# Other places for the Sinkhorn steps of the second mixture, and a branch hint for TensorE

## The chip, the cores and the metric

One core of a Trainium2 chip runs the whole program in one launch. The metric is the device time of that launch in microseconds, the median of several runs.

## The reference

Three layers follow each other, all in float32:

```
phi(x) = [exp(p - max|p|), exp(-(p - max|p|))],  p = x @ w_phi
x   = phi attention of q, k, v (2 batches, 8 heads, 576 tokens, 64 wide) -> 1152 tokens x 512
x   = moe(x):   each token goes to the expert of its largest logit, at most `capacity` of them
                per expert (288 here); out = gate * relu(x @ w1[e]) @ w2[e]; dropped tokens are 0
logits = x @ w_gate2;  P = exp(logits - logits.max())
for 8 rounds:  P /= P.sum(1) + 1e-9;  P /= P.sum(0) + 1e-9;  P *= N / E
out = sum over e of P[:, e] * (relu(x @ w1[e]) @ w2[e])      (8 experts, 512 -> 1024 -> 512)
```

The matrix products of the mixtures are done in float32 accuracy by splitting each operand into a high and a low part and adding three products.

## The kernel before

The order of the program is the order of the code: nothing reorders it, and each engine works through its own list.

**First mixture.** The loop over `jobs` handles one expert at a time. A branch on the expert's token count picks `job_wide` or `job_narrow` (the profile's input takes `job_narrow` in the last job). Each job lays its tokens in columns of `x2H` and `x2L`, so that the kept tokens stand together.

**Second mixture.** A last branch on the number of kept tokens, `with tc.If(kept_r > N - P)` (L1133), picks `moe2_all` or, here, `moe2_fast`, which works on the first 1024 columns only. The two bodies lie one behind the other in each engine's program.

`moe2_fast` goes through 32 *units*, four per expert, each a quarter of the expert's hidden columns. `first_plain` is unit 0: four groups of 12 matmuls (`three`, L198 to L200) make the hidden blocks; between them stand the gate's logits (`gate2`, L598 and L600, 24 matmuls), copied out by `sink_logits` (L829), and the two `mix` generators (L972 to L988), which make the sums and differences of the token blocks that the later units multiply. Then come the first four second-layer products of unit 0 (`second`, 6 matmuls each, one token tile of 128 each).

`unit(g)`, for g from 1 to 31, makes its hidden blocks by seven products `prod` (L995, 6 matmuls each) in a scheme with fewer multiplications, in three PSUM banks pA, pB, pC. After each product it calls `side(k)`, k from 0 to 6, and `side(7)` at the end. `side(k)` first issues one `second` of the unit before (only four of them in unit 1, at k from 0 to 3), then weight work (`prep2`, `prep`), then maybe a Sinkhorn step. VectorE and ScalarE turn the products into `hidH` and `hidL` (`relu_split`, L1030 and L1031).

The Sinkhorn work is a list `pending` of twelve steps, taken from the front: `sink_start` (nine transposes L839 on TensorE, then four small VectorE operations to the per-partition maximum), `sink_max` (transpose L848, then L849), `sink_exp` (small product L853, then L854, L855 and ScalarE's L856), `sink_row` (four VectorE operations, L859 to L862), and eight `sink_col` (product L867, L868, L869, then the next `sink_row`, or at the last the gate factor). Each step needs the one before, and the steps with a product make TensorE wait for VectorE. They are taken at t = 2 and 3 of `first_plain` and then at every odd k of `side`: two in unit 0, four in each of units 1 and 2, two in unit 3. The matrix `Pm` that they make is first used in unit 4, where the sums of expert 0 are scaled (`gates`).

Of the kernel before, what the change touches and what calls it, by code (L numbers as in the profile page):

```python
# [20 lines left out]
def kernel(  # L21
# [621 lines left out]
    with ExitStack() as mctx:  # L643
# [19 lines left out]
        def win_T(j, c):  # L663
# [5 lines left out]
                    ps[:, a * WP:(a + 1) * WP], xw[:, a, c * P:(c + 1) * P], ident[0:WP, 0:WP])  # L669
            split2(*x1[c], ps)  # L670

        def job_wide(j, off_r):
            i, w = jobs[j]
            for kk, f in enumerate(FO):
                ps = bank(W)
                for c in range(NC):
                    three(ps, wt.w1(f, c), x1[c], c, NC)
                evict_split(h1H[:, kk, :], h1L[:, kk, :], ps, relu=True)
                if i > 0 and kk < 4 and w == 0:
                    wt.split(i, 1, kk)  # L680
            pg = prep(0)
            for d in range(NC):
                ps = bank(W)
                for kk, f in enumerate(FO):
                    wH, wL = wt.w2(f)
                    three(ps, (wH[:, d * P:(d + 1) * P], wL[:, d * P:(d + 1) * P]),
                          (h1H[:, kk, :], h1L[:, kk, :]), kk, NFC)
                evict_split(x2H[:, d, ds(off_r, W)], x2L[:, d, ds(off_r, W)], ps)
                for c in ((0, 1), (2,), (3,), ())[d]:
                    win_T(j + 1, c)  # L690
                if d == 2:
                    win_load(j + 2)
                if w == NW - 1:
                    if i + 1 < E:
                        wt.split(i + 1, 0, d)
                    else:
                        next(pg)

        def job_narrow(j, off_r):
            i, w = jobs[j]  # L700
            pool = {(1, 3), (0, 1), (0, 3)}

            pg = prep(0)

            def split(i, which, p):
                if i == E:
                    next(pg)
                else:
                    wt.split(i, which, p, nc.gpsimd if (which, p) in pool else None)

            def turn_h(g):
                ps = bank4()
                for f in range(4):
                    o = f % 2 * P
                    nc.tensor.transpose(ps[:, f, :], hn[2 * g + f // 2][:, o:o + P], ident)
                split2(h1H[:, 4 * g:4 * g + 4, 0:P], h1L[:, 4 * g:4 * g + 4, 0:P], ps)

            if i > 0:
                split(i, 1, 0)
            for p in range(4):  # L720
                ps = bank(256)
                for c in range(NC):
                    three(ps, (x1[c][0][:, 0:P], x1[c][1][:, 0:P]), wt.w1p(p, c), c, NC)
                nc.scalar.activation(out=hn[p], in_=ps, func=AF.Relu)
                if i > 0 and p < 3:
                    split(i, 1, p + 1)
                if p == 1:
                    ring["n"] += 1
                if p == 2:
                    turn_h(0)  # L730
            win_T(j + 1, 0)
            win_T(j + 1, 1)
            turn_h(1)
            ring["n"] += 1
            split(i + 1, 0, 0)
            split(i + 1, 0, 1)
            for g in range(2):
                ps = bank(256)
                for kk, f in enumerate(FO):
                    wH, wL = wt.w2(f)  # L740
                    n = slice(g * 256, (g + 1) * 256)
                    three(ps, (h1H[:, kk, 0:P], h1L[:, kk, 0:P]), (wH[:, n], wL[:, n]), kk, NFC)
                nc.scalar.activation(out=yn[g], in_=ps, func=AF.Copy)
                if g == 0:
                    win_T(j + 1, 2)
                    split(i + 1, 0, 2)
            win_T(j + 1, 3)
            win_load(j + 2)
            ring["n"] += 1
            ps = bank4()  # L750
            for c in range(NC):
                o = c % 2 * P
                nc.tensor.transpose(ps[:, c, :], yn[c // 2][:, o:o + P], ident)
            split(i + 1, 0, 3)
            split2(x2H[:, :, ds(off_r, P)], x2L[:, :, ds(off_r, P)], ps)
# [180 lines left out]
    def moe2_fast(fp):  # L936
# [64 lines left out]
        def second(g, t):  # L1001
            e, p = divmod(g, 4)
            ps = pb[3 + nout[0] % 4]
            nout[0] += 1
            w = [sp1[2 * (g % 2) + x].rearrange("p (a n) -> p a n", a=2) for x in range(2)]
            n = slice(t % 4 * P, (t % 4 + 1) * P)
            for k in range(2):
                hH, hL = made[g][f"{k + 1}{t // 4 + 1}"]
                three(ps, (hH[:, n], hL[:, n]), (w[0][:, k, :], w[1][:, k, :]), k, 2)
            while gates and gates[0][0] <= nout[0]:  # L1010
                _, o, gate = gates.pop(0)
                nc.scalar.activation(out=o, in_=o, func=AF.Copy, scale=gate)
            o = oc[t]
            gate = Pm[:, t, e:e + 1]
            if g == 0:
                nc.scalar.copy(o, ps)
            elif e == 0:
                nc.vector.tensor_tensor(out=o, in0=ps, in1=o, op=ALU.add)
                if p == 3:
                    gates.append((nout[0] + 4, o, gate))  # L1020
            else:
                nc.vector.scalar_tensor_tensor(out=o, in0=ps, scalar=gate, in1=o, op0=ALU.mult, op1=ALU.add)  # L1022
            if g == 4 * E - 1:
                put(t)

        pending = [sink_start, sink_max, sink_exp, sink_row] + [lambda it=it: sink_col(it) for it in range(8)]

        def relu_split(dst, src):
            hi, lo = dst
# [4 lines left out]
        def first_plain():  # L1034
# [25 lines left out]
            for t in range(4):  # L1060
                second(0, t)
                if t < 2:
                    next(ms[1])
                else:
                    pending.pop(0)()
            return [slots[4], slots[5]]

        def unit(g, spare, todo):
# [10 lines left out]
            def side(k):  # L1079
                if todo:  # L1080
                    second(g - 1, todo.pop(0))
                if k == 0:
                    prep2(g)
                    if g + 1 < 4 * E:
                        pg[0] = prep(g + 1, stmp)
                if pg[0] and 1 <= k <= 4:
                    next(pg[0])
                    if k == 4:
                        wt.load(E + (g + 1) // 4 + 1, 0, (g + 1) % 4)
                if k % 2 and pending:  # L1090
                    pending.pop(0)()
                if g == 3 and k == 5:
                    for t in range(8, NT):
                        nc.gpsimd.memset(oc[t], 0.0)
                        put(t)
# [34 lines left out]
    def put(t):  # L1130
        scatter("out", out, tokc[:, t, 0:1], oc[t])

    with tc.If(kept_r > N - P) as cmp:  # L1133
        with tc.tile_pool(name="h2p", bufs=1) as h2p:
            moe2_all(h2p)
    with cmp.Else():
# [30 lines left out]
```

## Time and profile before

| what | value |
|---|---|
| median of 3 runs | 1029.74 us (1029.55 to 1030.85) |
| the profiled execution's own time | 1028.67 us |
| its span in the trace | 1027.0 us |
| mean granted clock of TensorE | 0.974 |
| busy: PE, DVE, ACT, POOL | 966.4, 604.6, 372.3, 412.9 us |

The stages in the profile's time: attention up to about 140 us, the first mixture from 147 to 337 us, the branch at 337 to 341 us, unit 0 to about 371 us, unit 1 to 394 us, unit 2 to 418 us, then about 20.4 us a unit to the end. PE is TensorE's matmuls, PEld its weight loads, DVE is VectorE, ACT ScalarE, POOL GpSimd. A time in brackets at a row's end is the idle time of the engine ahead of that row, with what ended it; "issue" means that nothing the profile shows was waited for.

### The profile page before, as it was taken

To read this page: it belongs to the slowest core of one execution; us is meant where nothing else is said; L and a number is where in the kernel's file an instruction comes from. 1 tells how busy PE (TensorE), PEld (TensorE's weight loads), DVE (VectorE), ACT (ScalarE), POOL (GpSimd) and SP (SyncE) were. 2 spreads that over 40 slices of the span, in tenths; PEclk is the share of its full clock that TensorE was granted. 3 is DMA by queue.
4 is the path that set the end of the run, shared out by engine and by line. 5 is a ranking of instruction groups with operands and counts; after the bars stand their busy time and mean duration, and the time that the engine had idled before them with its cause. 6 is when DMAs were issued, how large, how long until landed. Compare 5 with 4: busy or idle time off the path is not lost.

```text
span 1027.0 us, 14033 instructions
## 1 busy us (share of the span) xinstructions
PE 966.4 (94%) x5329; PEld 841.8 (82%) x5329; DVE 604.6 (59%) x1074; ACT 372.3 (36%) x621; POOL 412.9 (40%) x398
## 2 busy tenths in 40 slices
PE   8999969978888878999999999999999999999997
PEld 8999968968877656888888888888888888888886
DVE  4667764656554557855565556555655565556555
ACT  4456513566365332233223222322232223222320
POOL 2344243023033535435533553455345434543433
PEclk9999989999998889999999999999999999999999
DMA  7697121579686201111211221122112211110002
GB/s 125 150 276 236 62 89 31 179 212 241 200 230 192 79 21 62 51 41 56 68 42 41 61 63 42 41 62 62 41 41 62 63 41 42 61 41 1 1 1 82
DMA packets 123292, 89.68 MB, mean 87 GB/s; under 512 B 34528, under 2 KB 101344, under 8 KB 123200
## 3 DMA queue, kind: packets, MB, share of 16 engines
q1 hardware_dynamic: 120240, 83.65, 28.9%
q0 software_dynamic: 1728, 4.73, 1.2%
q8 instruction: 55, 0.90, 0.4%
q14 instruction: 37, 0.30, 0.1%
q10 hardware_dynamic: 1232, 0.10, 0.1%
HBM read 79.01 MB, written 9.45 MB: 86 GB/s over the span
## 4 chain that ended last, share of the span: by engine, by line
PE 80%; issue 8%; DVE 7%; ACT 2%; POOL 2%; DMA 1%; ACTq 0%; POOLq 0%; DVEq 0%; SPq 0%
PE pb L995 27%; PE pb L198 15%; PE pb L199 14%; PE pb L200 14%; PE pb L310 3%; PE pb L445 3%; PE pb L428 1%; POOL out_dram L177 1%; DVE hidL L1031 1%; PE pb L254 1%; PE pb L668 1%; DMA wg<-in_moe_w_gate_dram 0%; DVE w1L L158 0%; DVE x2L L801 0%; DVE dq L291 0%
## 5 line engine op out<-in xcount | busy, mean ns | idle before, releaser
L1022 DVE SCALAR_TENSOR_TENSOR oc<-pb,Pm,oc 128x512 f32<-128x512 f32 x224 | 167.1, 749 | 93.8 <-PE pb L200 91.5
L949 POOL TENSOR_TENSOR w1L<-raw,w1H 128x1024 fp32r<-128x1024 f32 x32 | 77.2, 2412 | 345.7 <-ACT w1H L948 345.7
L198 PE MATMUL pb<-w1H,hidH 128*128 128x512 f32 x512 | 199.8, 390 | 0.5 <-DVE hidL L1031 0.5
L199 PE MATMUL pb<-w1L,hidH 128*128 128x512 f32 x512 | 199.7, 390 | 0.0
L200 PE MATMUL pb<-w1H,hidL 128*128 128x512 f32 x512 | 199.6, 390 | 0.0
L1030 ACT ACTIVATE hidH<-snap 128x512 fp32r<-128x512 f32 x93 | 58.8, 632 | 240.7 <-DVE snap L1110 110.1
L995 PE MATMUL pb<-x2H,w0H 128*128 128x512 f32 x310 | 122.6, 396 | 0.0
L995 PE MATMUL pb<-x2L,w0H 128*128 128x512 f32 x310 | 121.7, 392 | 0.0
L995 PE MATMUL pb<-x2H,w0L 128*128 128x512 f32 x310 | 121.5, 392 | 0.0
L198 PEld LDWEIGHTS pb<-w1H,hidH 128*128 128x128 f32 x512 | 96.5, 189 | 20.7 <-DVE hidL L1031 0.6
L199 PEld LDWEIGHTS pb<-w1L,hidH 128*128 128x128 f32 x512 | 96.4, 188 | 20.1
L200 PEld LDWEIGHTS pb<-w1H,hidL 128*128 128x128 f32 x512 | 96.4, 188 | 20.1
L1031 DVE SCALAR_TENSOR_TENSOR hidL<-snap,hidH 128x512 fp32r<-128x512 f32 x93 | 65.7, 706 | 65.0 <-ACT hidH L1030 65.0
L640 POOL TENSOR_TENSOR w0L<-stmp,w0H 128x1024 fp32r<-128x1024 f32 x31 | 74.8, 2414 | 1.6 <-DMA raw<-in_moe_w_dram 1.6
L995 PEld LDWEIGHTS pb<-x2H,w0L 128*128 128x128 f32 x310 | 58.8, 190 | 12.4
L995 PEld LDWEIGHTS pb<-x2H,w0H 128*128 128x128 f32 x310 | 58.7, 189 | 11.9
L995 PEld LDWEIGHTS pb<-x2L,w0H 128*128 128x128 f32 x310 | 58.8, 190 | 11.8
L158 POOL TENSOR_TENSOR w1L<-raw,w1H 128x1024 fp32r<-128x1024 f32 x9 | 21.5, 2384 | 109.5 <-ACT w1H L155 109.2
L635 POOL TENSOR_TENSOR w0L<-raw,w0H 128x512 fp32r<-128x512 f32 x64 | 64.7, 1033 | 0.2 <-ACT w0H L624 0.2
L1030 ACT ACTIVATE hidH<-pb 128x512 fp32r<-128x512 f32 x35 | 20.9, 597 | 96.2 <-PE pb L995 91.3
L1098 ACT COPY snap<-pb 128x512 f32<-128x512 f32 x31 | 18.2, 587 | 83.7 <-PE pb L995 83.7
L995 PE MATMUL pb<-w1H,w0L 128*128 128x512 f32 x124 | 48.3, 389 | 0.0
(246 smaller groups left out, 1999.9 us busy)
## 6 DMA issues: line engine op xcount, KB each, us to landing
raw<-in_moe_w_dram SPq DMA_DIRECT2D x128, 256.0 KB, 3.5
raw<-in_moe_w_dram SPq DMA_DIRECT2D x64, 512.0 KB, 3.8
xe<-zero SPq DMA_DIRECT2D x18, 256.0 KB, 4.2
xw<-xe SPq DMA_DIRECT2D x7, 576.0 KB, 6.9
v<-in_v_dram SPq DMA_DIRECT2D x8, 256.0 KB, 4.9
q<-in_q_dram SPq DMA_DIRECT2D x8, 256.0 KB, 5.2
k<-in_k_dram SPq DMA_DIRECT2D x7, 256.0 KB, 4.9
xw<-xe SPq DMA_DIRECT2D x4, 144.0 KB, 2.5
```

The costliest lines, as they stand in the source:

```text
L198: nc.tensor.matmul(ps, lhsT=aH, rhs=bH, start=i == 0, stop=False)
L199: nc.tensor.matmul(ps, lhsT=aH, rhs=bL, start=False, stop=False)
L200: nc.tensor.matmul(ps, lhsT=aL, rhs=bH, start=False, stop=i == n - 1)
L310: nc.tensor.matmul(kvps[b][g // 4][:, g % 4, 0:MW], lhsT=kp[:, h, half, :], rhs=vv[:, h * VW:h * VW + MW], start=first and g % 4 == 0, sto ...
L445: nc.tensor.matmul(ps[:, h, 0:MW], lhsT=qt[:, g, :], rhs=kv[b][:, g * KW:g * KW + MW], start=half == 0, stop=half == 1,)
L635: tt(out=aL[:, o, :], in0=w, in1=aH[:, o, :].bitcast(F32), op=ALU.subtract)
L640: tt(out=sL, in0=wide(tmp), in1=sH.bitcast(F32), op=ALU.subtract)
L949: nc.gpsimd.tensor_tensor(out=lo, in0=r, in1=hi.bitcast(F32), op=ALU.subtract)
L995: nc.tensor.matmul(o, lhsT=a[x][:, c, :], rhs=b[c][y], start=first and c == 0 and m == 0, stop=c == 1 and m == 2, skip_group_check=True)
L1022: nc.vector.scalar_tensor_tensor(out=o, in0=ps, scalar=gate, in1=o, op0=ALU.mult, op1=ALU.add)
L1030: nc.scalar.activation(out=hi, in_=src, func=AF.Relu)
L1031: nc.vector.scalar_tensor_tensor(out=lo, in0=src, scalar=0.0, in1=hi.bitcast(F32), op0=ALU.max, op1=ALU.subtract)
```

## The change

First, the Sinkhorn steps are taken at twelve set places, pairs (unit, k) in a table `sink_at`, and no longer in `first_plain`. Second, the last branch gets a label, and at the head of the last job, in both of its bodies, TensorE is told which way that branch will go (a value computed from `kept_r`). An assertion says that the gate scaling comes after the last step.

```diff
@@ -669,8 +669,13 @@
                     ps[:, a * WP:(a + 1) * WP], xw[:, a, c * P:(c + 1) * P], ident[0:WP, 0:WP])
             split2(*x1[c], ps)
 
+        def hint(j):
+            if NW == 1 and j == len(jobs) - 1:
+                tc.mark_branch_hint_location("moe2", hint=kept_r > N - P, engines=[ENG.PE])
+
         def job_wide(j, off_r):
             i, w = jobs[j]
+            hint(j)
             for kk, f in enumerate(FO):
                 ps = bank(W)
                 for c in range(NC):
@@ -698,6 +703,7 @@
 
         def job_narrow(j, off_r):
             i, w = jobs[j]
+            hint(j)
             pool = {(1, 3), (0, 1), (0, 3)}
 
             pg = prep(0)
@@ -1009,6 +1015,7 @@
                 three(ps, (hH[:, n], hL[:, n]), (w[0][:, k, :], w[1][:, k, :]), k, 2)
             while gates and gates[0][0] <= nout[0]:
                 _, o, gate = gates.pop(0)
+                assert not pending
                 nc.scalar.activation(out=o, in_=o, func=AF.Copy, scale=gate)
             o = oc[t]
             gate = Pm[:, t, e:e + 1]
@@ -1024,6 +1031,7 @@
                 put(t)
 
         pending = [sink_start, sink_max, sink_exp, sink_row] + [lambda it=it: sink_col(it) for it in range(8)]
+        sink_at = ((1, 3), (1, 6), (2, 0), (2, 1), (2, 3), (2, 5), (2, 7), (3, 1), (3, 3), (3, 5), (3, 7), (4, 1))
 
         def relu_split(dst, src):
             hi, lo = dst
@@ -1061,8 +1069,6 @@
                 second(0, t)
                 if t < 2:
                     next(ms[1])
-                else:
-                    pending.pop(0)()
             return [slots[4], slots[5]]
 
         def unit(g, spare, todo):
@@ -1087,7 +1093,7 @@
                     next(pg[0])
                     if k == 4:
                         wt.load(E + (g + 1) // 4 + 1, 0, (g + 1) % 4)
-                if k % 2 and pending:
+                if (g, k) in sink_at:
                     pending.pop(0)()
                 if g == 3 and k == 5:
                     for t in range(8, NT):
@@ -1130,7 +1136,7 @@
     def put(t):
         scatter("out", out, tokc[:, t, 0:1], oc[t])
 
-    with tc.If(kept_r > N - P) as cmp:
+    with tc.If(kept_r > N - P, label="moe2") as cmp:
         with tc.tile_pool(name="h2p", bufs=1) as h2p:
             moe2_all(h2p)
     with cmp.Else():
```

What it moves, on TensorE and VectorE. At the head of the last narrow job TensorE's program reads before (pb is a PSUM bank, x1 the tokens, w0 the weights):

```order
L200 MATMUL pb_130<-h1H,w1L_157 128x288
L810 UNCONDITIONAL_BRANCH
L198 MATMUL pb_129<-w0H_142,x1H_1882 128x256
L199 MATMUL pb_129<-w0L_143,x1H_1882 128x256
L200 MATMUL pb_129<-w0H_142,x1L_1883 128x256
```

and now:

```order
L200 MATMUL pb_130<-h1H,w1L_157 128x288
L816 UNCONDITIONAL_BRANCH
L674 REGISTER_ALU
L1168 BRANCH_PREFETCH_HINT
L198 MATMUL pb_129<-w0H_142,x1H_1882 128x256
L199 MATMUL pb_129<-w0L_143,x1H_1882 128x256
L200 MATMUL pb_129<-w0H_142,x1L_1883 128x256
```

Two instructions more stand ahead of the job's first matmul; the other engines get none.

TensorE from the third second-layer product of unit 0 to the first product of unit 1, before (L839 the transposes of `sink_start`, L848 that of `sink_max`, hid the hidden blocks):

```order
L200 MATMUL pb_132<-w1H_150,hidL_10337 128x512
L839 MATMUL pb_133<-ident,l2s 128x16 x9
L198 MATMUL pb_129<-w1H_150,hidH_10332 128x512
L199 MATMUL pb_129<-w1L_151,hidH_10332 128x512
L200 MATMUL pb_129<-w1H_150,hidL_10333 128x512
L198 MATMUL pb_129<-w1H_150,hidH_10336 128x512
L199 MATMUL pb_129<-w1L_151,hidH_10336 128x512
L200 MATMUL pb_129<-w1H_150,hidL_10337 128x512
L848 MATMUL pb_133<-ident,gms 1x128
L995 MATMUL pb_126<-x2H,w0H_148 128x512
```

Now, at the end of unit 1's `side(3)` (the line numbers have moved by 6 there):

```order
L198 MATMUL pb_129<-w1H_150,hidH_10340 128x512
L199 MATMUL pb_129<-w1L_151,hidH_10340 128x512
L200 MATMUL pb_129<-w1H_150,hidL_10341 128x512
L845 MATMUL pb_133<-ident,l2s 128x16 x9
L1001 MATMUL pb_128<-x2H,w0H_146 128x512
```

and from the end of unit 1 (L854 is the old L848) into unit 2's `side(0)`:

```order
L1001 MATMUL pb_128<-x2H,w0L_147 128x512
L854 MATMUL pb_133<-ident,gms 1x128
L1001 MATMUL pb_126<-x2H,w0H_144 128x512
L1001 MATMUL pb_126<-x2L,w0H_144 128x512
L1001 MATMUL pb_126<-x2H,w0L_145 128x512
L1001 MATMUL pb_126<-x2H,w0H_144 128x512
L1001 MATMUL pb_126<-x2L,w0H_144 128x512
L1001 MATMUL pb_126<-x2H,w0L_145 128x512
L198 MATMUL pb_130<-w1H_152,hidH_10346 128x512
```

So the transposes stand four products of `prod` and five second-layer products later than before, and the second step is apart from the first by three products.

VectorE at the end of unit 0 and the start of unit 1, before:

```order
L194 TENSOR_TENSOR x2L<-snap_10344,x2H 128x2x256
L194 TENSOR_TENSOR x2L<-oc_5485,x2H 128x512
L841 COPY Pm<-pb_133 128x9x8
L842 TENSOR_TENSOR Pm<-Pm,pb_133 128x9x8
L834 TENSOR_TENSOR Pm<-Pm,tokc 128x9x8
L844 TENSOR_REDUCE gms<-Pm 128x1
L849 TENSOR_REDUCE gms<-pb_133 1x1
L1101 TENSOR_TENSOR snap_10345<-pb_127,snap_10344 128x512
L854 COPY gms<-pb_133 128x1
```

VectorE now, from the fourth product of unit 1 to the exponent in unit 2 (L840 and L850 are the old L834 and L844, L855 the old L849, L1039 the old L1031, L1025 the old L1018):

```order
L840 TENSOR_TENSOR Pm<-Pm,tokc 128x9x8
L850 TENSOR_REDUCE gms<-Pm 128x1
L1116 TENSOR_TENSOR snap_10352<-pb_128,snap_10352 128x512
L1039 SCALAR_TENSOR_TENSOR hidL_10339<-snap_10352,hidH_10338 128x512
L1120 TENSOR_TENSOR snap_10350<-pb_127,snap_10350 128x512
L1039 SCALAR_TENSOR_TENSOR hidL_10343<-snap_10350,hidH_10342 128x512
L1124 TENSOR_TENSOR snap_10351<-pb_128,snap_10351 128x512
L1039 SCALAR_TENSOR_TENSOR hidL_10349<-snap_10351,hidH_10348 128x512
L855 TENSOR_REDUCE gms<-pb_133 1x1
L1025 TENSOR_TENSOR oc_5484<-pb_130,oc_5484 128x512
L860 COPY gms<-pb_133 128x1
L861 TENSOR_SCALAR Pm<-Pm,gms 128x9x8
```

The four operations of the start stand among the splits of unit 1, and the reduction L855, for which TensorE waits, stands behind the last split of that unit.

## Rows read from the trace of the kernel before

**Rows 1.** Page, part 1: busy us of each engine, share of the span, instructions.

```profile
PE 966.4 (94%) x5329; PEld 841.8 (82%) x5329; DVE 604.6 (59%) x1074; ACT 372.3 (36%) x621; POOL 412.9 (40%) x398
```

**Rows 2.** Windows of TensorE: stretch, its length, PE busy (records), granted clock, DMA share, GB/s.

```profile
340.40:345.60 5.20, 5.16 (x12) 0.50 0.14 18
397.20:1024.00 626.80, 623.46 (x2755) 1.00 0.15 47
170.27:174.00 3.73, 3.42 (x18) 0.73 0.12 6
```

**Rows 3.** Waits of TensorE, 340 to 440 us: who for whom, us, times, longest.

```profile
PE pb L848 <- DVE gms L844: 6.4, 1, 6.4
PE pb L867 <- DVE cs L862: 4.4, 2, 3.9
```

**Rows 4.** Timeline, all engines, at the far branch: start, us, engine, line [idle before].

```profile
337.26 0.60 ACT L193 ACTIVATE x2H<-pb 128x512 f32 x1 [0.53 <-PE pb L753]
337.89 0.69 DVE L194 TENSOR_TENSOR x2L<-pb,x2H 128x512 f32 x1 [5.94 <-ACT x2H L193]
340.20 1.06 ACT L948 ACTIVATE w1H<-raw 128x1024 fp32r<-128x1024 f32 x1 [2.34 <-issue]
...
340.44 0.76 PE L198 MATMUL pb<-x2H,w0H 128*128 128x512 f32 x1 [3.21 <-issue]
```

**Rows 5.** Timeline, all engines, where the last job of the first mixture begins.

```profile
317.57 0.60 ACT L193 ACTIVATE x2H<-pb 128x512 f32 x1
...
318.05 1.07 ACT L155 ACTIVATE w1H<-raw 128x1024 fp32r<-128x1024 f32 x1
...
321.26 0.55 PE L198 MATMUL pb<-w0H,x1H 128*128 128x256 f32 x1 [4.33 <-DVE w1L L158]
```

**Rows 6.** Timeline of VectorE after the branch.

```profile
341.09 3.48 DVE L972 TENSOR_TENSOR snap<-x2H,x2L 128x512 f32<-128x512 f32 x2 [2.50 <-issue]
...
349.87 0.55 DVE L829 COPY l2s<-pb 16x384 f32<-16x384 f32 x1 [2.57 <-PE pb L600]
350.35 1.31 DVE L979 TENSOR_TENSOR oc<-snap,snap 128x512 f32<-128x512 f32 x1
...
352.84 0.69 DVE L981 TENSOR_TENSOR oc<-oc,oc 128x512 f32<-128x512 f32 x1
```

**Rows 7.** Chain that ended last, in order of time: start, us, what.

```profile
426.61 1.36 PE pb L995 x6
```

**Rows 8.** Timeline of TensorE: a stop in a job, then units 0 to 2.

```profile
170.27 0.29 PE L198 MATMUL pb<-h1H,w1H 128*128 128x288 f32 x1 [1.60 <-issue]
...
362.38 0.73 PE L839 MATMUL pb<-ident,l2s 16*128 16x16 f32 x9
363.60 0.50 PE L198 MATMUL pb<-w1H,hidH 128*128 128x512 f32 x1 [0.49 <-DVE hidL L1031]
...
379.72 0.38 PE L853 MATMUL pb<-gms,ones_f 1*128 1x1 f32 x2
...
398.60 0.39 PE L995 MATMUL pb<-w1H,w0H 128*128 128x512 f32 x1
```

**Rows 9.** Timeline of ScalarE at the start of unit 1.

```profile
366.75 0.57 ACT L1016 COPY oc<-pb 128x512 f32<-128x512 f32 x1
...
369.82 1.06 ACT L1016 COPY oc<-pb 128x512 f32<-128x512 f32 x2
374.61 0.59 ACT L1098 COPY snap<-pb 128x512 f32<-128x512 f32 x1 [3.72 <-PE pb L995]
```

**Rows 10.** Timeline of VectorE in unit 1.

```profile
372.05 0.28 DVE L849 TENSOR_REDUCE gms<-pb 1x1 f32<-1x128 f32 x1 [0.47 <-PE pb L848]
...
387.20 0.69 DVE L1110 TENSOR_TENSOR snap<-pb,snap 128x512 f32<-128x512 f32 x1 [0.82 <-PE pb L995]
388.59 1.87 DVE L1031 SCALAR_TENSOR_TENSOR hidL<-snap,hidH 128x512 fp32r<-128x512 f32 x1 [0.70 <-ACT hidH L1030]
...
391.76 0.69 DVE L1031 SCALAR_TENSOR_TENSOR hidL<-snap,hidH 128x512 fp32r<-128x512 f32 x1 [0.69 <-ACT hidH L1030]
```

## The prediction

> **What bounds the kernel now.** I read the busy shares first: TensorE works 94% of the span [rows 1], so time is won only where it stands still or runs slowly. The windows come next. From 397.2 us to the end TensorE is busy 623.46 of 626.8 us at a granted clock of 1.00 [rows 2]; whatever brings it to that stretch sooner moves the end by as much. The last list to read is that of its waits between 340 and 440 us: 6.4 us for the maximum that the Sinkhorn start needs (L848 waits for L844) and 4.4 us for column sums (L867 waits for L862, 3.9 of it at once) [rows 3]. Ahead of them stands a third hole, 3.21 us with no releaser, at the branch into the second mixture; the 12 matmuls after it took 5.2 us at a clock of 0.50, which is 1.2 GHz [rows 2, 4]. These three places are what the change touches.
>
> **What the hint costs.** It adds four rows to TensorE's program, two in each body of the last job, of which one pair runs. Before that job's first matmul TensorE waits 4.33 us for VectorE's L158 [rows 5]; the pair lies under that wait, so I cost it at nothing. Without that cover it would be two sequencer instructions, a fraction of a microsecond.
>
> **What the hint can give.** At the branch ScalarE stands 2.34 us and TensorE 3.21 us with nothing to wait for [rows 4]. VectorE stands 2.50 us [rows 6]. Between jobs ScalarE goes from the old body (L193, until 318.17) straight into the new one (L155, 318.05) [rows 5]; so not the branch itself is dear but the far body, whose code has to come. Removing TensorE's share does not give 3.2 us. Its first product needs x2H, written by 337.86, and its second x2L, written by 338.58 [rows 4]; with some 0.4 us from one product to the next it could begin at about 338.1 instead of 340.44, 2.4 us sooner. If the shorter hole of about 1 us leaves the clock at 2.4 GHz, the 12 matmuls take 2.7 us (six in 1.36) [rows 7] instead of 5.2, another 2.5. The nearest row for such a hole is the one of 1.60 us at 170.27, after which the clock averaged 0.73 [rows 2, 8], so this second part is doubtful.
>
> Who profits? VectorE waits for TensorE's logits (L829, 2.57 us of idle time, start 349.87) and is itself the chain from there on. Its two sums at L972 keep it until 344.57 and one L1031 until 345.3, since its own branch is not hinted [rows 6]. So L829 moves from 349.87 to between 345.3 and 347.5: 2.4 to 4.6 us. Part comes back: the differences L979 to L981 have both operands in SBUF and take 1.31 us at first and 0.69 at the last [rows 6]; moved earlier, all three fall beside GpSimd's weight work, which I price at 1.31 each, some 0.9 back. Net 1.5 to 3.7 us. I take **2.3**, nearer to the lower end because of the clock row.
>
> **What the Sinkhorn steps give.** Six-matmul products take 1.36 us [rows 7]. I follow TensorE without the old steps, on the old clock of events. The fourth second-layer product of unit 0 still waits for its bank until 363.60 [rows 8] and ends at 365.0. Now nothing stands ahead of unit 1's first product: 365.0 to 366.4 (before, L848 held it for 6.4 us). The next second-layer product needs a bank that ScalarE empties by 367.3 (L1016 at 366.75) [rows 9]: it ends at 368.7, the next pair at 371.4. The third product of unit 1 overwrites a bank that L1098 must first copy; that copy stands behind L1016, busy until 370.88, and takes 0.59 [rows 9], so it starts at 371.5 and ends at 372.9. Three products, the nine transposes of the start (0.73) [rows 8] and one more product bring 379.1.
>
> From there VectorE and ScalarE set the pace. The chain L1110, ScalarE, L1031, L1114, ScalarE, L1031 took from 387.20 to 392.45, 5.25 us, with one L1031 stretched to 1.87; L1118, ScalarE and a last L1031 add some 2.0 by the same rows, and L849 0.28 [rows 10]. It ends at 386.7. TensorE reaches the exponent's product (L853, now in unit 2) at about 384.9 and waits 1.8 us for it: the wait has not gone, it has shrunk. With 0.38 for L853 [rows 8] the second product of unit 2 starts at 387.1. Before, it started at 398.60 [rows 8]. That is 11.5 us. I take off 0.5 for one more step, at the head of unit 4, beside GpSimd's work; the steps in units 2 and 3, four or five a unit, cost what the four in unit 2 cost before, beside VectorE time that is off the path. Sum **11.0**. No DMA, no weight step and no POOL instruction changes its place; the exponential on ScalarE moves behind one weight copy and has two products' time.
>
> Sum: 11.0 + 2.3 = 13.3. The profiled execution took 1028.67, 1.07 below the median of the runs shown. So 1015.4 against it, and against the median 1029.74 - 13.3 = **1016.4**.
>
> **Rivals.** *The hint does nothing.* For: nothing in this trace shows a hinted branch, and the code to be fetched is the same. Against: from 321.26 to the branch TensorE has some 16 us of the last job in which it could be fetched [rows 4, 5]. Then 11.0 alone: 1018.7. The Trainium skill, "Runtime: NRT & Kernel Launch", section Instruction fetch mechanics, says that prefetch is purely sequential and that a taken branch to a target outside the window waits for a fetch; by that rule the hint is worth nothing and the time is 1018.7. On the stall itself the trace agrees with it (2.34 to 3.21 us at the far branch); whether a hint changes it no row shows.
>
> *The wait grows at its new place.* The exponent's product stands behind three relu splits on VectorE. If each L1031 there meets GpSimd as the one of 1.87 did [rows 10], 2.4 us come on top; a hole of over 3 us was followed by 1.2 GHz at the branch [rows 2, 4], which costs some 1.5 more over six matmuls. The gain falls to 9.4: about 1020.3.
>
> *Slower.* The armed target takes the place of the code that follows in line, and TensorE has to stop for its own last job. A stop would cost what the branch does, 3.2 us, and the slow matmuls after it 2.5. It decides from three such stops, 17 us against 13.3 us: 1029.74 + 3.8 = 1033.5. Against it: the largest stop in the middle of a job that I found is the 1.60 us of [rows 8], and the last job is short.
>
> **How the numbers follow.** A measurement of this kernel tells about 0.2%, 2.1 us, from no change. Forecast 0.55; hint without effect 0.25; wait grown 0.12; slower 0.04; the rest, 0.04, is split between a better outcome and a gain lost to something unseen. Faster is 0.94, same 0.02, slower 0.04. The low end takes 3.7 for the hint and 1.2 more if L1031 escapes GpSimd: a gain of 15.9, 1013.8, which I round to 1013.5. The high end is the hint at nothing and the clock fallen at the new wait, a gain of 8.5 or so: 1021.
>
> **What would show it.** Right: L848 and L867 leave TensorE's waits or stay under 1 us each; the hole at the branch falls from 3.21 to about 1 us while ScalarE and VectorE keep theirs; L853 waits 1 to 2 us; unit 2's second product starts near 385; nothing else moves. If the hole stays at 3.2, the hint failed. If unit 2 starts near 385 and the end does not follow, the reading of the last 627 us was wrong. If L867 shows new waits in units 2 to 4, the spacing of the steps was.

## The result and the profile after

The changed kernel took 1015.22 us (median of 4 runs, 1012.88 to 1020.01), the kernel before 1029.89 us beside it (4 runs, 1029.55 to 1030.85). The ratio is 0.9875 with a 95% interval of 0.9847 to 0.9903, so the change saves 10 to 16 us. The profiled execution took 1013.54 us, with a span of 1011.8 us and a mean granted clock of 0.98.

The page's first part; it answers to [rows 1]:

```profile
PE 960.1 (95%) x5329; PEld 836.6 (83%) x5329; DVE 607.2 (60%) x1074; ACT 371.6 (37%) x621; POOL 415.4 (41%) x398
```

The same number of instructions on every engine, 6.3 us less of busy time on TensorE: part of the gain is matmuls that now run at the full clock. Where it stood still shows in its waits from 330 us on (who for whom, us in total, times, longest), which answer to [rows 3]:

```profile
PE pb L198 <- ACT oc L1023: 2.3, 1, 2.3
PE pb L198 <- DVE hidL L1039: 1.5, 1, 1.5
PE pb L198 <- ACT x2H L193: 1.3, 1, 1.3
PE pb L859 <- DVE gms L855: 1.0, 1, 1.0
PE pb L873 <- DVE cs L868: 0.5, 1, 0.5
```

The 6.4 us of L848 (now L854) and the 3.9 us of L867 (now L873) are gone; one wait of 0.5 us for column sums is left, as before. In their place stand 2.3 us for a bank that ScalarE's copy L1023 empties and 1.0 us at the exponent's product L859; the wait for a bank that VectorE's split L1039 empties grew from 0.5 to 1.5 us.

The timeline of all engines at the far branch, which answers to [rows 4]:

```profile
334.26 0.44 PE L759 MATMUL pb<-ident,yn 128*128 128x128 f32 x2 [0.26 <-ACT yn L749]
334.74 0.60 ACT L193 ACTIVATE x2H<-pb 128x512 f32 x1 [0.53 <-PE pb L759]
...
336.01 0.47 PE L198 MATMUL pb<-x2H,w0H 128*128 128x512 f32 x1 [1.31 <-ACT x2H L193]
...
338.21 1.06 ACT L954 ACTIVATE w1H<-raw 128x1024 fp32r<-128x1024 f32 x1 [2.88 <-issue]
...
338.90 3.52 DVE L978 TENSOR_TENSOR snap<-x2H,x2L 128x512 f32<-128x512 f32 x2 [2.85 <-issue]
```

TensorE's hole shrank from 3.21 to 1.31 us, and the row now names a releaser, x2H of L193. That isn't all of it: x2H was written by 335.34, and the product began 0.67 us later. In the second profile of the change, where the hole is 0.78 us, it began 0.15 us after x2H. What the other half microsecond is shows below, where the fetches are read. ScalarE and VectorE still stand for 2.9 us with nothing to wait for. Windows of TensorE (first the length, then each engine's busy time with its records, the granted clock behind POOL):

```profile
336.00:338.90 2.90, 2.89 (x13) 2.36 (x14) 0.06 (x1) 0.69 (x1) 0.00 (x0) 1.00 0.39 107
...
362.30:368.00 5.70, 5.70 (x18) 4.57 (x19) 3.53 (x6) 4.98 (x9) 0.21 (x1) 0.70 0.01 3
382.90:1009.00 626.10, 622.63 (x2753) 515.10 (x2752) 377.35 (x569) 179.62 (x275) 289.01 (x252) 1.00 0.15 47
```

The matmuls behind the branch run at a clock of 1.00 (2.4 GHz) where [rows 2] had 0.50. The last 626 us are as they were.

**A measure for what follows.** The first mixture doesn't end at the same time in every execution: the last pair of its transposes (L753, now L759) started between 331.47 and 338.49 us in the profiles of this study. This spread is there before TensorE comes to the hint: the transposes of the job ahead of the last one started between 311.16 and 318.02 us, at 316.10 and 312.05 in two kernels without the hint (before, and the steps alone) and at 313.62 after the change. So the 2.5 us that the last pair came sooner (334.26 against 336.79) aren't taken as the change's gain. I compare the **stretch**: from the start of that pair to the end of the span. It took 690.2 us before (1027.0 - 336.79) and 677.5 us after (1011.8 - 334.26), 12.7 less. Ratios are each to the kernel before on the same chip, whose own median lay between 1023.7 and 1029.9 us.

### The profile page after: what moved, and what is told of

Same layout as the page of the kernel before. It is cut to its first block, busy times and chain, and to the rows that moved or that the text cites. A ratio compares the mean times of both kernels' runs of the same rounds, so it can differ in the third digit from the quotient of the medians.

```text
span 1011.8 us, 14034 instructions
## 1 busy us (share of the span) xinstructions
PE 960.1 (95%) x5329; PEld 836.6 (83%) x5329; DVE 607.2 (60%) x1074; ACT 371.6 (37%) x621; POOL 415.4 (41%) x398
## 4 chain that ended last, share of the span: by engine, by line
PE 79%; issue 8%; DVE 7%; ACT 2%; DMA 2%; POOL 2%; ACTq 0%; POOLq 0%; DVEq 0%; SPq 0%
PE pb L1001 27%; PE pb L198 14%; PE pb L199 14%; PE pb L200 14%; PE pb L310 3%; PE pb L445 3%; PE pb L428 1%; DMA raw<-in_moe_w_dram 1%; PE pb L668 1%; DVE hidL L1039 1%; POOL out_dram L177 1%; DVE snap L978 1%; PE pb L254 1%; DMA wg<-in_moe_w_gate_dram 1%; DVE w1L L158 0%
## 5 line engine op out<-in xcount | busy, mean ns | idle before, releaser
L955 POOL TENSOR_TENSOR w1L<-raw,w1H 128x1024 fp32r<-128x1024 f32 x32 | 77.0, 2408 | 336.1 <-ACT w1H L954 336.1
L200 PE MATMUL pb<-w1H,hidL 128*128 128x512 f32 x512 | 199.3, 389 | 0.0
L1001 PE MATMUL pb<-x2H,w0H 128*128 128x512 f32 x310 | 121.6, 392 | 0.0
L1001 PE MATMUL pb<-x2L,w0H 128*128 128x512 f32 x310 | 120.7, 389 | 0.0
L1001 PE MATMUL pb<-x2H,w0L 128*128 128x512 f32 x310 | 120.6, 389 | 0.0
L200 PEld LDWEIGHTS pb<-w1H,hidL 128*128 128x128 f32 x512 | 96.2, 188 | 20.0
L1039 DVE SCALAR_TENSOR_TENSOR hidL<-snap,hidH 128x512 fp32r<-128x512 f32 x93 | 64.6, 695 | 64.9 <-ACT hidH L1038 64.9
L1001 PEld LDWEIGHTS pb<-x2H,w0L 128*128 128x128 f32 x310 | 58.2, 188 | 12.2
L1001 PEld LDWEIGHTS pb<-x2H,w0H 128*128 128x128 f32 x310 | 58.2, 188 | 11.9
L1001 PEld LDWEIGHTS pb<-x2L,w0H 128*128 128x128 f32 x310 | 58.2, 188 | 11.8
L158 POOL TENSOR_TENSOR w1L<-raw,w1H 128x1024 fp32r<-128x1024 f32 x9 | 21.7, 2409 | 109.6 <-ACT w1H L155 109.2
L1001 PE MATMUL pb<-w1H,w0H 128*128 128x512 f32 x124 | 48.8, 394 | 0.0
L1001 PE MATMUL pb<-w1L,w0H 128*128 128x512 f32 x124 | 48.7, 393 | 0.0
```

Of the source, the lines that this page charges most:

```text
L200: nc.tensor.matmul(ps, lhsT=aL, rhs=bH, start=False, stop=i == n - 1)
L955: nc.gpsimd.tensor_tensor(out=lo, in0=r, in1=hi.bitcast(F32), op=ALU.subtract)
L1001: nc.tensor.matmul(o, lhsT=a[x][:, c, :], rhs=b[c][y], start=first and c == 0 and m == 0, stop=c == 1 and m == 2, skip_group_check=True)
L1039: nc.vector.scalar_tensor_tensor(out=lo, in0=src, scalar=0.0, in1=hi.bitcast(F32), op0=ALU.max, op1=ALU.subtract)
```

## The experiments

All of them first. "Hole" is TensorE's idle time ahead of its first product behind the branch; hole and stretch are those of one profile each.

| kernel | ratio to before, 95% interval | hole, us | stretch, us |
|---|---|---|---|
| before | 1 | 3.21 | 690.2 |
| the change | 0.9875 (0.9847 to 0.9903) | 1.31 | 677.5 |
| the change again | 0.9870 (0.9846 to 0.9894) | 0.78 | 677.0 |
| steps alone | 0.9901 (0.9878 to 0.9923) | 3.34 | 679.8 |
| hint alone | 0.9979 (0.9963 to 0.9996) | 0.78 | 687.7 |
| hint for three engines | 0.9873 (0.9849 to 0.9898) | 0.78 | 677.6 |
| hint inverted | 0.9878 (0.9830 to 0.9927) | 3.84 | 679.8 |
| hint 1.1 us ahead of the branch | 0.9890 (0.9839 to 0.9941) | 3.54 | 680.4 |
| hint 4 us ahead | 0.9874 (0.9834 to 0.9913) | 0.89 | 678.0 |
| hint 7 us ahead | 0.9879 (0.9845 to 0.9913) | 0.78 | 677.1 |
| unit 0's copies first | 0.9859 (0.9807 to 0.9912) | 1.31 | 676.3 |
| steps of unit 1 sooner | 0.9863 (0.9815 to 0.9911) | 0.78 | 676.8 |
| both | 0.9860 (0.9813 to 0.9908) | 0.78 | 676.0 |
| both, later steps spread anew | 0.9894 (0.9842 to 0.9946) | 0.78 | 679.3 |

The ratios tell the steps from nothing, and just tell the hint from nothing; 1 us is below what they can tell, and there the stretch of one profile speaks, with that reserve.

### The two parts apart

Steps alone: the hint is never issued.

```diff
-            if NW == 1 and j == len(jobs) - 1:
+            if False:
```

> The Sinkhorn steps at their set places, no hint. Theory A (the two parts add up: about 11 us from the steps, the rest from the hint): TensorE stands some 3 us at the far branch with 1.2 GHz after it, L848's wait is gone, L859 waits about 1 to 2 us; 11 us faster than before, near 1019. Rival B (the steps carry all, the hint nothing): as fast as the full change, near 1015. Rival C (the steps only move their waits and the hint carries the gain): less than 5 us faster.

Hint alone: the steps are taken where they were before.

```diff
                 if t < 2:
                     next(ms[1])
+                else:
+                    pending.pop(0)()
...
-                if (g, k) in sink_at:
+                if k % 2 and pending:
                     pending.pop(0)()
```

> The hint alone, Sinkhorn steps where they stood. Theory A: the hole at the branch falls to about 1.3 us, VectorE's chain behind it moves by 2 to 3 us, and L848's wait on TensorE grows by what TensorE came earlier, since VectorE sets it: 2 to 3 us faster, near 1027. Rival B: no change, hole of 3 us. Rival C: over 8 us faster.

The change again, unaltered, on the same chip:

> The full change once more, unaltered, beside the others. Its four runs lay between 1012.88 and 1020.01 us, those of before within 1.3. If the spread comes from the first mixture's transfers, TensorE's last matmul before the branch falls at different times and the stretch from the branch to the end stays within 1 us of 677.5 us; the median stays near 1015. If it comes from the hint (sometimes in time, sometimes not), the hole at the branch differs from run to run.

The stretch is 10.4 us shorter with the steps alone and 2.5 us with the hint alone; the sum of 12.9 lies between the two profiles of the full change, 12.7 and 13.2. Within that half microsecond the parts add. The change again shows what its spread comes from: the holes of the two profiles do differ, but by 0.53 us only, and the stretch by 0.5, while the first mixture ended 2.8 us sooner (331.47 against 334.26). The windows behind the branch, first of steps alone, then of hint alone:

```profile
336.30:341.50 5.20, 5.19 (x12) 3.92 (x13) 3.47 (x2) 1.03 (x1) 4.09 (x3) 0.50 0.14 27
```

```profile
333.20:336.10 2.90, 2.73 (x11) 2.04 (x12) 0.56 (x1) 0.00 (x0) 0.00 (x0) 1.00 0.52 149
```

Without the hint the 12 matmuls are as slow as in [rows 2]; with it, 11 records take half the time. And yet the hint alone hardly pays. Its waits of TensorE:

```profile
PE pb L854 <- DVE gms L850: 8.0, 1, 8.0
PE pb L873 <- DVE cs L868: 3.9, 1, 3.9
```

Counted from the last pair of transposes, TensorE comes to this maximum 4.1 us sooner than before, VectorE delivers it only 2.6 us sooner, and so the wait of 6.4 us grows to 8.0. What counts is how much sooner VectorE is done with unit 0, and that is told below.

### Which code is fetched, and when

The hint for the other two engines too:

```diff
-hint=kept_r > N - P, engines=[ENG.PE])
+hint=kept_r > N - P, engines=[ENG.PE, ENG.Activation, ENG.DVE])
```

> The full change with the same hint for ScalarE and VectorE too, whose stops at the branch were 2.88 and 2.85 us with the change. Theory A: their stops fall under 1 us, but VectorE then waits for TensorE's logits (L835, at 342.6 in the changed kernel's trace, before at 342.95), so at most 1 to 2 us more than the full change, through less meeting of VectorE and GpSimd. Rival: if VectorE's branch is what holds the chain, 2.8 us more, near 1012.

The hint with the wrong answer, so that the instructions and their places stay and only the armed direction is another:

```diff
-hint=kept_r > N - P, engines=[ENG.PE])
+hint=kept_r <= N - P, engines=[ENG.PE])
```

> The full change with the hint's value turned round. Theory A (the hint works because the far body's code is fetched during the last job): TensorE's hole at the branch is back at 3 us or longer, with 1.2 GHz after it, and the stretch from the last transpose of the first mixture to the end is that of the steps alone, 679.8 us, or up to 3 us longer if a wrong hint costs a fetch. Rival B (not the fetch but the two added instructions or the shifted code changed the hole): the hole stays near 1 us, 677 us.

The timeline with the wrong answer:

```profile
334.12 0.44 PE L759 MATMUL pb<-ident,yn 128*128 128x128 f32 x2 [0.26 <-ACT yn L749]
...
338.39 0.47 PE L198 MATMUL pb<-x2H,w0H 128*128 128x512 f32 x1 [3.84 <-issue]
```

The hole is back, with no releaser, and the stretch (679.8 us) is that of the steps alone. So it is the direction that is told which takes the stop away, not the two instructions more nor where the code lies. (The 1.2 GHz of the expectation came in part: the first three matmuls behind the hole ran at a clock of 1.00, the rest at 0.50 to 0.56.) Its ratio, 0.9878, doesn't show this loss: 2 us drown in the spread between runs.

With all three engines hinted, ScalarE has no stop left, but VectorE's stays. Both the theory and its rival start from VectorE's stop, so neither was tested:

```profile
336.47 0.60 ACT L193 ACTIVATE x2H<-pb 128x512 f32 x1 [0.53 <-PE pb L759]
...
337.01 1.06 ACT L954 ACTIVATE w1H<-raw 128x1024 fp32r<-128x1024 f32 x1
...
340.14 2.66 DVE L978 TENSOR_TENSOR snap<-x2H,x2L 128x512 f32<-128x512 f32 x2 [2.35 <-issue]
```

The stretch (677.6) is no shorter, but not because nothing moved. VectorE needed 20.85 us from L835 to its last split of unit 0 (21.90 in the change), and unit 2's second product began 47.05 us after the last pair, against 48.6 in the change and 48.0 in the change again. Just ahead of that product TensorE waited 1.68 us at L859, as long as in the change again. Windows of TensorE behind this wait, with three engines hinted and in the change again:

```profile
382.70:384.70 2.00, 2.00 (x6) 1.71 (x7) 1.96 (x3) 0.45 (x1) 1.47 (x1) 0.54 0.01 4
```

```profile
379.20:381.20 2.00, 2.00 (x10) 1.68 (x10) 1.96 (x3) 0.43 (x1) 1.49 (x1) 1.00 0.01 4
```

Behind the same wait the clock was 0.54 in the one and 1.00 in the other, and what was won was lost there: from that product to the end it took 630.5 us against 629.0.

How early must it be said? The change says it at the head of the last job, some 16 us ahead of the branch. Three kernels say it later (their edit for the other body of the job, which doesn't run, is left out here). First just ahead of the job's transposes, which begin 1.1 us before the last of them ends:

```diff
 def job_narrow(j, off_r):
     i, w = jobs[j]
-    hint(j)
...
     ring["n"] += 1
+    hint(j)
     ps = bank4()
     for c in range(NC):
```

> The full change, but the hint for TensorE is issued late in the job, just ahead of its last transposes, instead of at the job's head. Theory (the hint starts the fetch of the far code, which takes as long as the stop of 3.3 us without it): part of the stop stays, between 1.3 and 3.3 us idle of TensorE at the branch, and the stretch from the last transpose to the end takes 678 to 679.8 us. Rival (a hint at any time ahead of the branch is enough): TensorE idles 0.8 to 1.3 us there as in the full change, and the stretch takes 677.0 to 677.6 us.

```profile
337.44 0.44 PE L760 MATMUL pb<-ident,yn 128*128 128x128 f32 x2 [0.26 <-ACT yn L749]
...
341.41 0.77 PE L198 MATMUL pb<-x2H,w0H 128*128 128x512 f32 x1 [3.54 <-issue]
```

Both theories missed: not a part of the stop stayed but all of it, 3.54 us, and the stretch of 680.4 us is that of no hint. A fetch that begins at the hint would have had a start of 1.1 us. So I put the hint between the two places:

```diff
+    hint(j)
     for g in range(2):
         ps = bank(256)
```

> The full change with the hint ahead of the last job's second-layer products, some 7 us ahead of the branch instead of 16 (1.2 us ahead, the stop stayed at 3.54 us). Theory (the far code comes from the hint on, and takes about as long as the stop, 3.3 us, so 7 us are enough): TensorE idles 0.8 to 1.3 us at the branch, and the stretch from the last transpose to the end takes 677.0 to 677.6 us. Rival (the hint is acted on late, and needs most of the job): 3.2 us or more stay, and the stretch takes 679.8 us or more.

```diff
     for g in range(2):
+        if g == 1:
+            hint(j)
         ps = bank(256)
```

> The same with the hint ahead of the second half of those products, some 4 us ahead of the branch. Theory (the fetch takes about 3.3 us from the hint on): 0.8 to 1.3 us idle of TensorE at the branch, and 677.0 to 677.6 us for the stretch. Rival (a hint needs clearly more than the stop's own time, between 4 and 16 us): 2 us or more stay, and the stretch takes 679 us or more.

The timelines of these two, first 7 us, then 4 us ahead (in the second the second half of those products starts at 330.30 and the transposes end at 334.23):

```profile
335.25 0.47 PE L198 MATMUL pb<-x2H,w0H 128*128 128x512 f32 x1 [0.78 <-ACT x2H L193]
```

```profile
335.12 0.47 PE L198 MATMUL pb<-x2H,w0H 128*128 128x512 f32 x1 [0.89 <-ACT x2H L193]
```

4 us are enough for the hole, 1.1 us gain nothing. A fetch that begins at the hint and takes as long as the stop, 3.2 to 3.8 us, doesn't explain that, since then 1.1 us would have saved 1.1 us.

The traces show the fetches themselves. The view of the DMA queues lists two queues of instructions; q8 is TensorE's, by its pace: in the last 627 us it moves a packet of 16 KB every 28.8 us, and in that time TensorE works off some 254 matmuls and weight loads, far more than all other engines together. Packets, MB and share of q8 over the whole program, before and in the change again:

```profile
q8 instruction: 55, 0.90, 0.4%
```

```profile
q8 instruction: 54, 0.88, 0.4%
```

Every kernel without a hint, with the wrong one or with the late one has 55, every other one 54. Narrow windows of that view give the time at which a packet starts. Counted in us from the last pair of transposes:

| kernel | packet ahead of the branch | packet in the hole | first product |
|---|---|---|---|
| before | -2.0 | 0.9 | 3.65 |
| steps alone | -2.0 | 0.9 | 3.78 |
| hint inverted | -1.8 | 1.6 | 4.27 |
| hint 1.1 us ahead | -2.5 | 1.3 | 3.97 |
| the change | -0.8 | none | 1.75 |
| unit 0's copies first | -0.8 | none | 1.74 |
| hint 4 us ahead | -1.2 | none | 1.33 |
| the change again | -1.5 | none | 1.22 |
| hint 7 us ahead | -2.0 | none | 1.21 |
| the five others with a hint | -1.4 to -2.0 | none | 1.21 to 1.22 |

With no useful hint a packet has to come in the hole, and the first product starts 2.7 to 2.9 us after that packet does. With a useful hint this packet is missing; the one ahead of the branch goes at about the same time whether the hint stands 16, 7 or 4 us ahead. So no fetch of the hint's own shows; that the hint decides which code the next packet brings is a reading of these rows, not shown by them. It fits the holes that are left: with the packet at -0.8 or -1.2 the first product came 2.5 us after it (holes of 1.31 and 0.89 us), with the packet at -1.4 or earlier it waited for the data alone (0.78 us). And it fits the late hint: there the packet had started 1.9 us before TensorE began the transposes that stand behind the hint. No row shows when the hint itself was taken, nor what sets the packet off, so how early is early enough stays open between 1.1 and 4 us.

The 678.0 us of the kernel with 4 us, 1.0 more than with 7, are not the hint's. VectorE, which has no hint, stood 3.21 us at the branch there against 2.64; its copy of the logits came 9.05 us after the last pair against 8.51, and TensorE's product behind L1025 (the change's L1023) 28.38 us after it against 27.83. The other 0.4 us are the clock: behind that wait of 2.34 us it fell to 0.77 and then 0.65 in the one and stayed at 1.00 in the other.

### The waits that are left

The 2.3 us for ScalarE's L1023: in unit 0 the second-layer products, with the copies that empty their banks, come before the last work of the mixing generators.

```diff
-            next(ms[1])
-            next(ms[0])
             wt.load(E + 1, 0, 1)
             for t in range(4):
                 second(0, t)
-                if t < 2:
-                    next(ms[1])
+            next(ms[1])
+            next(ms[0])
+            next(ms[1])
+            next(ms[1])
```

> The full change, with unit 0's four second-layer products and ScalarE's copies of them ahead of the second half of mix, so that the copies no longer stand behind splits that wait for VectorE. Theory A (the bound at unit 1's head is ScalarE's order, TensorE waits 2.35 us for L1023): that wait goes, the third product comes sooner, 1.5 to 2.5 us less, 675 us from the last transpose to the end. Rival (VectorE's chain through mix and the splits of unit 1 sets it anyway): TensorE waits as long at another row, below 0.5 us.

The 1.0 to 1.7 us at the exponent: the two steps of unit 1 come sooner.

```diff
-        sink_at = ((1, 3), (1, 6), (2, 0), ...
+        sink_at = ((1, 2), (1, 4), (2, 0), ...
```

> The full change, with the first step at side 2 and the second at side 4 of unit 1 in place of 3 and 6. Theory A (TensorE's wait of 1.0 to 1.7 us at L859 comes from L855 standing behind the last split of unit 1 on VectorE): the wait goes, 1 to 1.7 us less, near 675.8 us. Rival (the splits themselves are late, so that the product after it waits for them): the same wait one product on, 677 us.

Both edits together:

> The two orders of the two runs before this together. Theory A: they add up, 2.5 to 4 us less than the full change, near 673.7 us from the last transpose to the end. Rival: the gain of the better of the two, near 675.

Waits of TensorE from 340 us on, of copies first, of the steps sooner, and of both:

```profile
PE pb L859 <- DVE gms L855: 1.7, 1, 1.7
...
PE pb L1001 <- ACT snap L1104: 1.1, 1, 1.1
```

```profile
PE pb L198 <- ACT oc L1023: 2.3, 1, 2.3
PE pb L873 <- DVE cs L868: 1.6, 2, 1.1
```

```profile
PE pb L873 <- DVE cs L868: 1.6, 2, 1.1
...
PE pb L1001 <- ACT snap L1104: 1.2, 1, 1.2
```

Each edit takes its wait away, and each time another comes up behind it: the copy L1104 at unit 1's third product, the column sums at the step (2,7). The stretches, 676.3, 676.8 and 676.0 us, are 0.2 to 1.5 us shorter than those of the two profiles of the change, which differ by 0.5 themselves; none came down to what its Theory A gave (675, 675.8 and 673.7). The last idea was that the 1.1 us at (2,7) come from the spacing alone:

```diff
-sink_at = ((1, 3), (1, 6), (2, 0), (2, 1), (2, 3), (2, 5), (2, 7), (3, 1), (3, 3), (3, 5), (3, 7), (4, 1))
+sink_at = ((1, 2), (1, 4), (2, 0), (2, 1), (2, 3), (2, 5), (3, 0), (3, 2), (3, 4), (3, 6), (4, 0), (4, 2))
```

> Unit 0's copies first and the steps of unit 1 sooner, as in the run with both, and the steps behind them spread anew over units 2 to 4, at (2,0), (2,1), (2,3), (2,5), (3,0), (3,2), (3,4), (3,6), (4,0), (4,2). Theory (the 1.1 us that TensorE waits at L873 at (2,7) is spacing alone): that wait goes, and the stretch from the last transpose of the first mixture to the end takes 675.0 us instead of 676.0. Rival (VectorE has no room left in units 1 and 2): the wait comes back at another step or at the second product, 0.8 us or more in all, and the stretch stays at 676.0 or above.

TensorE, GpSimd and VectorE there:

```profile
427.97 0.39 PE L873 MATMUL pb<-cs,ones_f 128*128 128x8 f32 x2 [3.18 <-DVE cs L868]
```

```profile
425.16 2.33 POOL L955 TENSOR_TENSOR w1L<-raw,w1H 128x1024 fp32r<-128x1024 f32 x1 [9.80 <-ACT w1H L954]
```

```profile
425.44 2.14 DVE L867 TENSOR_TENSOR Pm<-Pm,rs 128x72 f32<-128x72 f32 x1
427.62 0.29 DVE L868 TENSOR_REDUCE cs<-Pm 128x8 f32<-128x80 f32 x1
```

The rival's signs came: the wait is back at another step, larger (3.18 us), the clock behind it was 0.60 from 427.9 to 430.0 us, and the stretch is 3.3 us longer than with both. A scaling of 72 elements per partition (L867), which took 0.23 us at its fastest in this trace, took 2.14 us beside GpSimd's weight work L955 (425.16 to 427.49): it ended when GpSimd did. The Trainium skill ("SBUF — State Buffer", section SBUF: two separate sides) says that a VectorE operation with two SBUF inputs and a GpSimd operation that reads SBUF exclude each other for a whole instruction; these rows agree, 427.58 against 427.49 us. The change has such a scaling too (2.37 us from 404.75), and there TensorE waited 0.5 us only: VectorE began that step 2.6 us after the step's product (401.15 to 403.73), in this run 4.1 us after it (420.30 to 424.42). So the wait has two parts, VectorE's other work ahead of the step and GpSimd's beside it, and a step's place isn't only a matter of distance to the step before. None of these versions is shown to beat the change: all their intervals overlap its own.

## Why the prediction was right

The forecast of 1016.4 us stands beside 1015.22 measured, and the range held it. What was forecast is a gain of 13.3 us; the stretch gave 12.7 and 13.2 us in the two profiles of the change. The medians differ by 14.7 us; the 1.5 to 2 us beyond the stretch come from the part ahead of the last transposes, whose spread the forecast knows nothing of. Step by step, with times counted from the start of the last transposes of the same profile:

**The hint works** (forecast: hole about 1 us; measured 1.31 and 0.78). The rival that it does nothing falls by the inverted hint. The rule of the Trainium skill ("Runtime: NRT & Kernel Launch", section Instruction fetch mechanics) that prefetch is purely sequential would have left the hole at 3.21 us; the runs differ from it, 0.78 to 1.31 us with a hint 4 us or more ahead of the branch. Its other half, that a taken branch to a far target waits for a fetch, agrees with the 3.34 and 3.84 us of the unhinted and the wrongly hinted branch, in both of which a packet of TensorE's code comes in the hole.

**The clock** stayed at 1.00 behind the shorter hole in every profile that has one; the doubt that I drew from the row of 1.60 us was not borne out there (behind other waits of 1.68 and 2.34 us it was, in some profiles). So L835 (the old L829) came 8.69 us after the transposes instead of 13.08: 4.4 us sooner, near the top of my 2.4 to 4.6. What bounds it in the change is VectorE, as I had worked out for that end: L835 follows VectorE's own split without a wait.

**The give-back was sized too low.** I took 0.9 us for the differences beside GpSimd. From L835 to the last split of unit 0 VectorE needed 20.08 us before (349.87 to 369.95) and 21.90 now. The rows that differ most, before:

```profile
351.76 1.04 DVE L980 TENSOR_TENSOR snap<-oc,snap 128x512 f32<-128x512 f32 x1
...
356.04 0.68 DVE L194 TENSOR_TENSOR w1L<-snap,w1H 128x512 fp32r<-128x512 f32 x1
...
358.95 3.99 DVE L972 TENSOR_TENSOR snap<-x2H,x2L 128x512 f32<-128x512 f32 x2
...
363.46 0.67 DVE L979 TENSOR_TENSOR oc<-snap,snap 128x512 f32<-128x512 f32 x1
...
369.95 0.69 DVE L194 TENSOR_TENSOR x2L<-oc,x2H 128x512 fp32r<-128x512 f32 x1 [0.31 <-ACT x2H L193]
```

and after:

```profile
343.41 0.71 DVE L985 TENSOR_TENSOR oc<-snap,snap 128x512 f32<-128x512 f32 x1
344.23 1.59 DVE L986 TENSOR_TENSOR snap<-oc,snap 128x512 f32<-128x512 f32 x1
345.86 1.11 DVE L987 TENSOR_TENSOR oc<-oc,oc 128x512 f32<-128x512 f32 x1
...
349.94 1.78 DVE L194 TENSOR_TENSOR w1L<-snap,w1H 128x512 fp32r<-128x512 f32 x1
...
353.39 2.87 DVE L978 TENSOR_TENSOR snap<-x2H,x2L 128x512 f32<-128x512 f32 x2
...
356.78 2.26 DVE L985 TENSOR_TENSOR oc<-snap,snap 128x512 f32<-128x512 f32 x1
...
364.85 0.69 DVE L194 TENSOR_TENSOR x2L<-oc,x2H 128x512 fp32r<-128x512 f32 x1 [0.31 <-ACT x2H L193]
```

The three differences that I counted gave back less than I took: 3.41 us (0.71, 1.59, 1.11) against 3.04 before (1.31, 1.04, 0.69 [rows 6]), 0.4 us. The rest is what I had left out: the second L985 took 1.6 us more and the split L194 of w1L 1.1 us more, each beside an operation of GpSimd, while the second pair of sums L978 (the old L972) took 1.1 us less. So 4.4 - 1.8 = 2.6 us against the 2.3 I took: the move of L835 and the give-back were both sized too low, and the two misses nearly cancel, which is luck. Hint alone gave 2.5.

**The steps** came to 10.4 us alone, forecast 11.0. The path went as worked out: in the run with the steps alone the second-layer product behind the copy L1023 started 30.59 us after the transposes (forecast 367.3 - 336.79 = 30.5), L859 waited 1.67 us (1.8), and the second product of unit 2 began after 50.8 us, before after 61.8: 11.0 where I had 11.5. The 0.5 us that I took off on top, for a collision at (4,1), was the right size for the wrong reason: no such wait came (TensorE's only wait for column sums is the old 0.5 us). But two column sums more now stand behind that product, and each costs TensorE time without any wait. Its timeline at one of them:

```profile
396.60 0.39 PE L200 MATMUL pb<-w1H,hidL 128*128 128x512 f32 x1
396.82 0.28 PE L873 MATMUL pb<-cs,ones_f 128*128 128x8 f32 x2
396.96 0.48 PE L1001 MATMUL pb<-x2H,w0H 128*128 128x512 f32 x1
397.27 0.40 PE L1001 MATMUL pb<-x2L,w0H 128*128 128x512 f32 x1
```

Matmuls follow each other by 0.23 us; from L200 to the second L1001 it is 0.67 us instead of 0.46. Two such steps make 0.4 of the 0.6 us by which the rest of the program is longer (1012.3 - 383.32 = 629.0 against 1027.0 - 398.60 = 628.4).

**Where the hint's share goes.** With the hint TensorE starts the fourth second-layer product of unit 0 4.2 us sooner than in the run with the steps alone, and then waits 2.34 us instead of 0.75 for L1023, since that copy hangs on VectorE's chain, 2.6 us sooner only. That is the reading "VectorE is the chain from there on", and why 4.2 us on TensorE are worth 2.5.

**The last 627 us** followed: unit 2's second product started 48.6 us (again: 48.0) after the transposes, forecast 384.8 - 336.79 = 48.0.

**The other rivals.** The wait at its new place stayed at 1.0 to 1.7 us and did not grow to 4.2. TensorE did not stop for its own last job either, and no cost of the hint shows there: from the transposes of the job before it to its own last pair it took 20.64 us (313.62 to 334.26), before 20.69 (316.10 to 336.79). In the profiles with the hint at the job's head this stretch took 20.1 to 22.1 us, in those without 20.5 and 20.7, so a cost below that spread isn't ruled out. The wait for L158 under which I put the pair was 4.70 us.

## What to carry to other kernels

Where TensorE stands for some 3 us at a far branch with nothing to wait for, tell it the direction 4 us or more ahead (ScalarE's hint worked too, VectorE's did not), and value it by what the next engine in the chain gains, not by the hole. Take a chain of small dependent steps off a place where the engine that sets the end must wait, put them where other work lies between two of them, and count the small matmuls themselves (0.2 us each step) against the gain. When such waits are down to 1 us each, the next one stands right behind.

## What the hardware showed that was not expected

- A hint 1.1 us ahead of the branch saved nothing of a stop of 3.5 us, one 4 us ahead all but 0.89 us. The packet of TensorE's code that goes ahead of the branch starts 0.8 to 2.0 us ahead of the last pair of transposes in the kernels with a hint in time, whether it stands 16, 7 or 4 us ahead.
- The hint for VectorE had no effect (2.35 us of stop left) where that for ScalarE took 2.9 us to nothing; why stays open.
- Waits of the same length were followed by different clocks. Behind the 2.34 to 2.35 us for L1023 it was 0.70 in one profile of the change (362.3 to 368.0 us) and 1.00 in the other; behind 1.68 us at L859 it was 0.54 with three engines hinted and 1.00 in the change again. The first cost 0.4 us, since the wait behind it shrank from 1.68 to 0.99 us; the second cost 1.5 us.
